# A top-k attention and MLP kernel: AV one slot later and behind the score products, the norm at the end of even slots, the MLP weights one slot later

## The chip, the cores and the metric

The kernel runs on one core of a Trainium2 chip. A core has a matrix engine (PE, or TensorE, with its weight loads shown as PEld), VectorE (DVE), ScalarE (ACT), GpSimd (POOL) and SyncE (SP), which only issues DMAs here. Each engine works through its own instructions in the order of the program and waits on semaphores for the others. The metric is the time of the whole program on the device, in microseconds (us).

## The reference: what is computed

Eight batches of eight heads, sequence 576, head dimension 64. Each row of scores keeps its 32 largest entries, softmax runs over those, and the result is multiplied by v. The eight heads side by side (512 columns) go through a two-layer MLP with a leaky activation whose slope is learned per column.

```python
scores = scale * np.matmul(q, k.transpose(0, 1, 3, 2))
kth = np.partition(scores, -top_k, axis=-1)[..., -top_k:-top_k + 1]
scores = np.where(scores >= kth, scores, -1000000000.0)
attn = np.exp(scores - np.max(scores, axis=-1, keepdims=True))
attn = attn / (np.sum(attn, axis=-1, keepdims=True) + 1e-09)
x = np.matmul(attn, v)          # (8, 8, 576, 64), then heads side by side: (4608, 512)
h = x @ w_in                    # (512, 2048)
g = np.maximum(h, 0.0) + alpha * np.minimum(h, 0.0)
out = g @ w_out                 # (2048, 512)
```

## The kernel before

Two heads make a pair (32 pairs, four to a batch). Work is cut into 144 **duos**. A normal duo is 128 rows of q of both heads of a pair, that is 256 rows of 576 scores in a tile s of 128 partitions x 2 x 576. A mixed duo takes the 64 rows left at the end of two pairs; two of each eighteen duos of a batch are mixed (the list is built at lines 77 to 85).

The main loop (line 719) goes through **slots** n = 0 to 147. Each slot emits one stage of several duos, so that a duo passes through the engines over some eight slots. The order of the calls in the loop body is the order in which each engine finds its work; nothing reorders it, apart from DVE's smallest instructions.

- Slot n computes the score products of duo n+1 on PE (`st_qk`, line 233) into the one score tile of PSUM, and ACT copies them out (`st_exit`, line 255, called the exit).
- DVE finds the eight largest of each sixth of the rows of duo n (`dve_slot`, line 313: twelve MAX8 per duo). In odd slots it folds them into a lower threshold for the two duos of the slot pair (`threshold_steps`, line 285).
- ACT takes the sign of duo n−2's scores against that threshold and counts (`st_count`), POOL makes y from it (`st_y`), and DVE takes the eight next candidates of each row from y (`row`, line 282). In even slots three small steps (`pick_steps`, line 265) pick the exact threshold of the pair two before.
- ACT and POOL then push the scores below the threshold of duo n−4 far down (`st_relu`), ACT takes exp of duo n−5 into w, and SP starts a transposing DMA of w into wT (`st_exp`, line 419 on); wT has three buffers.
- PE multiplies wT with v (`st_av`, line 426): ten matmuls for a normal duo, twenty for a mixed one. Column 64 of v is one, so that the row sums come out beside the product. The result of an even duo and the odd one behind it share the tile xo, of which there is **one** (`ps_x`, line 101). In the slot table (line 381 on) AV stands six slots behind the duo's own; it is called late in the loop body (line 751), behind the MLP part `o_pe` and the transposes of the next q and k (`prep`).
- The norm of a pair of duos (line 451) is a reciprocal of the row sums (`norm_a`) and a multiply that writes x in bf16 (`norm_b`). It is done in even slots, for the duos n−8 and n−7 (`norm_of`, line 260). Within the slot it goes: the twelve maxima with the pick steps between them, one MLP evacuation (`h_dve`), `norm_a`, first rows of y, `norm_b`, second rows. `norm_b` frees xo for the next AV, which in an even slot is that of duo n−6.
- Behind the loop body SP transposes a finished x into xT (`st_xT`), and from two slots later the MLP takes it: `h_pe` emits one unit of the first layer, at the head of a slot, `o_pe` a part of the second. Where there is no such unit, `keep_warm` (line 557, `rest` in the profile) multiplies zeros in its place.

The MLP's weights come in during the first slots: four loads of w_out and four of w_in by POOL's queue (lines 656 to 658), scaled copies of w_out by alpha on ACT and DVE (`scale_out`, line 660), transposes of w_in by SP (`in_trans`), and a product of the two (`lin`, `lin_out`) in slots 15 to 23. The first MLP unit needs the second of these products, the first output all four. All of that goes by a table of slots (`at`).

DMAs are issued in order on each queue: SP has the loads of q, k and v, the transposes of w, x and w_in, and the stores; POOL has the weights.

Of the kernel before, what the change touches and what calls it, by code (L numbers as in the profile page):

```python
# [59 lines left out]
def fast_path(tc, q, k, v, moe_w_in, moe_w_out, moe_alpha, out, flag):  # L60
# [17 lines left out]
    for b in range(B):  # L78
        p0 = KPB * b
        last = b == B - 1  # L80
# [3 lines left out]
    ND = len(duos)  # L84
# [3 lines left out]
    with ExitStack() as ctx:  # L88
# [91 lines left out]
        def at(slot, kind, f):  # L180
            todo.setdefault((max(0, slot), kind), []).append(f)
# [100 lines left out]
        def row(d, i):  # L282
            DVE.max(out=T["p9", d // 2][:, 2 * (d % 2) + i, 1:9], in_=T["y", d][:, i, :])
# [29 lines left out]
        def dve_slot(n, f_late):  # L313

            norm = norm_of(n)
            rows = [d for d in duos_at("row", n)]
            picks = [f for m in duos_at("pick", n) for f in pick_steps(m)]
            if on(n):
                s = T["s", n]
                if n % 2 == 0:  # L320
                    T["up", n // 2] = two.tile([128, 4, NG // 2, 8], FP32, name="up", tag="up")
                up = T["up", n // 2]
                for i in range(2):
                    r = 2 * (n % 2) + i
                    for g in range(NG):
                        o = 24 * r + 8 * (g // 2)
                        m = DVE.max(out=(lo if g % 2 else up)[:, r, g // 2, :],
                                    in_=s[:, i, GW * g:GW * g + GW])
                        if g % 2:
                            sm(m, [], [(o, o + 8)])  # L330
                            if picks:
                                picks.pop(0)()
                if n % 2 == 0:
                    h_dve()
                    if norm:
                        norm_a(norm)
                    for d in rows:
                        row(d, 0)
                    if norm:
                        norm_b(norm)  # L340
                    for d in rows:
                        row(d, 1)
                else:
                    fold, negate, least, turn = threshold_steps(n // 2)
                    fold()
                    h_dve()
                    negate()
                    for d in rows:
                        row(d, 0)
                    least()  # L350
                    turn()
                    for d in rows:
                        row(d, 1)
            else:
                if norm:
                    norm_a(norm)
                    norm_b(norm)
                early = picks and duos_at("pick", n)[0] < ND // 2 - 1
                if early:
                    for f in picks:  # L360
                        f()
                if not norm:
                    h_dve()
                for d in rows:
                    row(d, 0)
                    row(d, 1)
                if not early:
                    for f in picks:
                        f()
                if norm:  # L370
                    h_dve()
            if f_late:
                h_pe()
                h_dve()

        stage = {}

        def duos_at(kind, n):
            return stage.get((kind, n), [])

        for d in range(ND):
            last = d - (ND - 4) if d >= ND - 4 else None
            for kind, lag, drain in (("count", 2, (2, 2, 2, 1)), ("relu", 4, (4, 3, 3, 2)),
                                     ("exp", 5, (5, 4, 4, 3)), ("av", 6, (6, 5, 5, 4))):
                stage.setdefault((kind, d + (lag if last is None else drain[last])), []).append(d)
        for (kind, n), l in list(stage.items()):
            if kind == "count":
                stage["row", n] = l
# [174 lines left out]
        def h_dve():  # L563
            if act:
                ch, f0, e_n, ph = act.pop(0)
                DVE.tensor_scalar(ch["g"][:, f0:f0 + e_n, :], ph, 0.0, None, ALU.max)
                ch["done"] += e_n
# [48 lines left out]
        def w_in_load(i):  # L616
            POOL.dma_start(w_in_b[i], moe_w_in[128 * i:128 * i + 128, :])
# [3 lines left out]
        def out_load(i):  # L621
            hold["st", i] = gp.tile([128, 4, DMODEL], FP32, name="w_st", tag="gT")
            POOL.dma_start(hold["st", i], moe_w_out[512 * i:512 * i + 512, :].rearrange("(f p) n -> p f n", p=128))

        def scale_out(f):
            if f % 8 == 0:
                hold["wl", f // 8] = gp.tile([128, 8, 512], BF16, name="w_la", tag="gT")
            src = hold["st", f // 4][:, f % 4, :]
            ACT.activation(w_out_b[f // 4][:, f % 4, :], src, AF.Copy, scale=alpha1m[:, f:f + 1])

            sm(DVE.tensor_tensor(hold["wl", f // 8][:, f % 8, :], src,
                                 alpha_ps[:, f:f + 1].to_broadcast([128, 512]), ALU.mult),
               [(304 + f, 305 + f)], [])

        def in_trans(kk):
            if kk % 2 == 0:
                hold["wi", kk // 2] = gp.tile([128, NFT, 256], BF16, name="w_inT", tag="gT")
            SP.dma_start_transpose(hold["wi", kk // 2][:, :, 128 * (kk % 2):128 * (kk % 2) + 128], w_in_b[kk])
# [11 lines left out]
        def lin_out(kk):  # L650
            ACT.copy(w_lin_b[kk], hold["z"])
            if kk == 3:
                lin_done.append(1)


        for i in range(4):
            at((1, 3, 5, 8)[i], "w", lambda i=i: out_load(i))
            at((4, 7, 10, 12)[i], "w", lambda i=i: w_in_load(i))
        for f in range(NFT):
            at((3, 3, 4, 4, 5, 6, 7, 7, 8, 9, 10, 11, 11, 12, 13, 14)[f], "scale", lambda f=f: scale_out(f))  # L660
        for kk in range(4):
            at((11, 12, 15, 17)[kk], "ld", lambda kk=kk: in_trans(kk))
            for a in range(2):
                at(15 + 2 * kk + a, "lin", lambda kk=kk, a=a: lin(kk, a))
            at(17 + 2 * kk, "lin_out", lambda kk=kk: lin_out(kk))

        def run(n, kind, most=99):
            l = todo.get((n, kind), [])
# [50 lines left out]
        for n in range(ND + 4):  # L719
            end = n >= ND  # L720
            now[0] = n
            run(n, "ld")
            o_sp()

            if end:
                for m in duos_at("av", n):
                    st_av(m)
            if not h_pe() and not end:
                keep_warm()
            if n and on(n + 1):  # L730
                st_qk(n + 1)
            late = len(hq) > (9 if n < 118 else 4) and n % 2 == 0 or end

            for m in duos_at("count", n):
                st_count(m)
                st_y(m)
            for m in duos_at("exp", n):
                st_exp(m)
            did = o_pe()
            run(n, "w")  # L740

            dve_slot(n, late)
            for m in duos_at("relu", n):
                st_relu(m, 0)
                st_relu(m, 1)
            if on(n + 1):
                st_exit(n + 1)
            run(n, "cast")
            run(n, "lin_out")
            run(n, "prep", 2 if n < 4 else 1)  # L750
            if not end:
                for m in duos_at("av", n):
                    st_av(m)
            if end or ready() > 4 or all(len(d.shape) == 3 for d, _ in pend):
                o_act()
            if (n, "lin") in todo:
                run(n, "lin")
            else:
                late_o[0] = 0 if end else 1
                if not (end or ready() > 2) or not o_pe():  # L760
                    if not end and not did:
                        keep_warm()
                late_o[0] = 0
            while pend:
                short = len(pend[0][0].shape) == 3
                wide = pend[0][0].shape[1] == 512
                on_dve = short and n > 16 or wide and (n < 17 or n % 2 == 0)
                prep_evac(DVE.tensor_copy if on_dve else ACT.copy)
            if n == 1:
                sm(DVE.tensor_copy(alpha_ps, aps), [], [(304, 320)])  # L770
                ACT.activation(alpha1m, aps, AF.Copy, scale=-1.0, bias=1.0)
            run(n, "scale")
            if norm_of(n):
                st_xT(norm_of(n) - 1)
                st_xT(norm_of(n))
            if n == ND + 3:
                check_low()
# [294 lines left out]
```

## Time and profile before

| | us |
|---|---|
| median of three runs | 882.73 |
| lowest and highest of them | 881.53, 884.63 |
| the profiled execution's own time | 883.55 |
| its span in the profile | 881.3 |

| engine | busy us | share of the span |
|---|---|---|
| PE | 773.3 | 88% |
| DVE | 764.1 | 87% |
| ACT | 765.5 | 87% |
| POOL | 755.6 | 86% |

The mean granted clock of PE is 0.943 of full speed. A row of the timeline gives the start, the duration, the engine, the operation with what it writes and reads, how many instructions are merged in it, and in brackets how long the engine was idle before it and what ended that. A row of waits gives who waited for whom, the total, how often, and the longest. In a row of stretches each engine's busy time is followed by the count of its instructions, and then come the granted clock, the DMA engines' busy share and their GB/s. Every instruction carries the line of a helper (L32), so that groups are told apart by the tiles' names: ps_sc are the score products, s_sb the exits (by ACT) or the scores, xo is AV, x the norm's product, KZ<-xo its reciprocal, ph and gT the first MLP layer, pz the second, tps the transposes of q and k, rest the fillers.

### The profile page before, as it was taken

Reading aid. Unit: us, or ns where it says so; the run is one execution under the profiler, and the core shown is the slowest. Engines: PE = TensorE matmul, PEld = TensorE weight load, DVE = VectorE, ACT = ScalarE, POOL = GpSimd, SP = SyncE. Lnnn points to the kernel's source line nnn. Section 1 sums busy time; section 2 is a strip of 40 time slices with the busy share of each in tenths; the row PEclk is TensorE's granted clock in tenths of the full one; section 3 lists DMA queues with packets and bytes.
Section 4 is the critical chain, followed back from the end, with each engine's and each line's share of the span. In section 5 each row is a group of like instructions: output and inputs, shape, how many; then the busy total and the mean of one; then the engine's idle time right before and its main releaser. Section 6 shows DMA issues by size and latency. Waiting matters only on the chain.

```text
span 881.3 us, 17690 instructions
## 1 busy us (share of the span) xinstructions
PE 773.3 (88%) x5299; PEld 438.1 (50%) x5386; DVE 764.1 (87%) x3475; ACT 765.5 (87%) x1255; POOL 755.6 (86%) x708
## 2 busy tenths in 40 slices
PE   7858698988999889899989889899989989889887
PEld 4323254555555555455545555555545555445454
DVE  2889698999998989999997989999997989999832
ACT  3679699999998999999998989999997988998930
POOL 1589699999998999999898889999998888998930
PEclk9979799999999999997998999999998999989989
DMA  7587866556655556565554455656555554443341
GB/s 169 122 160 161 159 110 130 101 115 127 112 117 113 111 92 142 113 126 115 111 120 100 104 110 127 120 124 127 116 114 116 105 106 99 84 83 71 80 96 40
DMA packets 344167, 100.19 MB, mean 114 GB/s; under 512 B 338032, under 2 KB 338048, under 8 KB 344064
## 3 DMA queue, kind: packets, MB, share of 16 engines
q1 hardware_dynamic: 340992, 91.87, 52.1%
q0 software_dynamic: 1872, 6.82, 3.3%
q8 instruction: 44, 0.72, 0.4%
q14 instruction: 59, 0.48, 0.2%
q10 hardware_dynamic: 1200, 0.30, 0.2%
HBM read 36.71 MB, written 9.44 MB: 52 GB/s over the span
## 4 chain that ended last, share of the span: by engine, by line
PE 36%; DVE 29%; ACT 14%; POOL 10%; issue 5%; DMA 4%; SPq 1%; ACTq 0%; POOLq 0%
PE ps_sc L32 10%; PE pz L32 10%; DVE small L32 9%; DVE p L32 7%; PE ph L32 7%; DVE up L32 5%; PE xo L32 5%; POOL s_sb L32 5%; POOL y L32 4%; ACT sg L32 4%; ACT s_sb L32 4%; DVE gT L32 3%; PE rest L32 3%; ACT r L32 3%; ACT w L32 2%
## 5 line engine op out<-in xcount | busy, mean ns | idle before, releaser
L32 POOL TENSOR_TENSOR y<-s_sb,sg 128x576 f32<-128x576 f32 x288 | 361.9, 1277 | 89.6 <-ACT sg L32 88.8
L32 POOL TENSOR_TENSOR s_sb<-s_sb,r 128x576 f32<-128x576 f32 x288 | 362.0, 1277 | 1.6 <-ACT r L32 1.5
L32 DVE MAX8 up<-s_sb 128x8 f32<-128x96 f32 x864 | 212.6, 246 | 18.9 <-ACT s_sb L32 18.4
L32 ACT ACTIVATE sg<-s_sb,p 128x576 bf16<-128x576 f32 x288 | 221.1, 772 | 5.4 <-DVE p L32 4.9
L32 DVE MAX8 p<-y 128x8 f32<-128x576 f32 x288 | 215.2, 747 | 10.2 <-POOL y L32 9.7
L32 DVE MAX8 small<-s_sb 128x8 f32<-128x96 f32 x864 | 216.6, 251 | 0.0
L32 ACT COPY s_sb<-ps_sc 128x1152 f32<-128x1152 f32 x144 | 159.5, 1108 | 60.1 <-PE ps_sc L32 59.1
L32 ACT ACTIVATE r<-s_sb,KZ 128x576 bf16<-128x576 f32 x288 | 205.9, 765 | 0.0
L32 PE MATMUL ps_sc<-qkT 64*128 64x512 f32 (+2 forms) x768 | 186.1, 583 | 3.5 <-ACT s_sb L32 3.5
L32 PE MATMUL xo<-v,wT 128*128 128x65 bf16 (+3 forms) x1600 | 129.0, 201 | 67.7 <-DVE x L32 47.1
L32 ACT ACTIVATE w<-s_sb 128x1152 bf16<-128x1152 f32 x144 | 166.2, 1154 | 6.2 <-POOL s_sb L32 6.0
L32 PE MATMUL ph<-xT,w_in_b 128*128 128x256 bf16 (+1 forms) x1408 | 161.4, 265 | 0.9 <-PE xo L32 0.5
L32 PE MATMUL pz<-w_out_b,gT 128*128 128x512 bf16 x557 | 152.3, 396 | 5.6 <-issue 3.2
L32 PEld LDWEIGHTS <-wT 128*128 128x128 bf16 (+3 forms) x1600 | 97.4, 101 | 113.2 <-issue 57.4
L32 PEld LDWEIGHTS <-w_in_b 128*128 128x128 bf16 x1408 | 121.5, 103 | 38.0 <-issue 9.5
L32 DVE TENSOR_SCALAR gT<-ph 128x512 bf16<-128x512 f32 x144 | 97.7, 679 | 36.9 <-PE ph L32 36.2
L32 PEld LDWEIGHTS <-gT 128*128 128x128 bf16 x576 | 57.7, 100 | 65.3 <-issue 15.0
L32 PEld LDWEIGHTS ps_sc<-kd,qkT 128*128 128x128 f32 x256 | 38.4, 189 | 100.6 <-issue 99.0
L32 PEld LDWEIGHTS ps_sc<-qkT 64*128 64x128 f32 (+1 forms) x768 | 54.8, 175 | 59.3 <-issue 43.1
L32 PE MATMUL rest<-idle 128*128 128x512 bf16 x209 | 62.7, 421 | 4.7 <-DVE qkT L32 2.7
L32 PE MATMUL ps_sc<-kd,qkT 128*128 128x128 f32 x256 | 62.9, 328 | 0.0
L32 ACT ACTIVATION_READ_ACCUMULATOR sg<-s_sb,p 128x1 f32 x288 | 55.7, 193 | 0.0
(57 smaller groups left out, 558.8 us busy)
## 6 DMA issues: line engine op xcount, KB each, us to landing
k_st<-in_k_dram SPq DMA_DIRECT2D x64, 128.0 KB, 2.9
v_st<-in_v_dram SPq DMA_DIRECT2D x64, 128.0 KB, 2.8
q_st<-in_q_dram SPq DMA_DIRECT2D x62, 128.0 KB, 2.7
out_dram<-o_sb SPq DMA_DIRECT2D x31, 256.0 KB, 2.5
w_st<-in_moe_w_out_dram POOLq DMA_DIRECT2D x4, 1024.0 KB, 6.6
wT<-w SPq DMA_TRANSPOSE x144, 3.5
w_in_b<-in_moe_w_in_dram POOLq DMA_DIRECT2D x4, 512.0 KB, 6.2
k_st<-in_k_dram SPq DMA_DIRECT2D x32, 32.0 KB, 3.1
```

What stands on the lines that cost most here:

```text
L32: ins = self.tc.keep_in_program_order(f(*a, **kw))
```

## The change

AV of a duo stands seven slots behind the duo instead of six, and is called right behind the score products of the next duo, ahead of everything else that PE does in the slot from there on. The AV of an odd duo, n−7, thus comes in the even slot n, that of the next even duo in the odd slot n+1. The last four duos keep their slots, and no AV of the others goes beyond slot 145. In even slots DVE does the first rows of y, then `norm_a`, the second rows, then `norm_b`. All table entries of the weights (loads, scaled copies, transposes, product) go up by one slot; the slot of the norm and the MLP's own rules stay.

```diff
                 if n % 2 == 0:
                     h_dve()
+                    for d in rows:
+                        row(d, 0)
                     if norm:
                         norm_a(norm)
                     for d in rows:
-                        row(d, 0)
+                        row(d, 1)
                     if norm:
                         norm_b(norm)
-                    for d in rows:
-                        row(d, 1)
...
-                                     ("exp", 5, (5, 4, 4, 3)), ("av", 6, (6, 5, 5, 4))):
-                stage.setdefault((kind, d + (lag if last is None else drain[last])), []).append(d)
+                                     ("exp", 5, (5, 4, 4, 3)), ("av", 7, (6, 5, 5, 4))):
+                at_slot = d + (lag if last is None else drain[last])
+                if d < ND - 4:
+                    at_slot = min(at_slot, ND + 1)
+                stage.setdefault((kind, at_slot), []).append(d)
...
-            at((1, 3, 5, 8)[i], "w", lambda i=i: out_load(i))
-            at((4, 7, 10, 12)[i], "w", lambda i=i: w_in_load(i))
+            at((2, 4, 6, 9)[i], "w", lambda i=i: out_load(i))
+            at((5, 8, 11, 13)[i], "w", lambda i=i: w_in_load(i))
         for f in range(NFT):
-            at((3, 3, 4, 4, 5, 6, 7, 7, 8, 9, 10, 11, 11, 12, 13, 14)[f], "scale", lambda f=f: scale_out(f))
+            at((4, 4, 5, 5, 6, 7, 8, 8, 9, 10, 11, 12, 12, 13, 14, 15)[f], "scale", lambda f=f: scale_out(f))
         for kk in range(4):
-            at((11, 12, 15, 17)[kk], "ld", lambda kk=kk: in_trans(kk))
+            at((12, 13, 16, 18)[kk], "ld", lambda kk=kk: in_trans(kk))
             for a in range(2):
-                at(15 + 2 * kk + a, "lin", lambda kk=kk, a=a: lin(kk, a))
-            at(17 + 2 * kk, "lin_out", lambda kk=kk: lin_out(kk))
+                at(16 + 2 * kk + a, "lin", lambda kk=kk, a=a: lin(kk, a))
+            at(18 + 2 * kk, "lin_out", lambda kk=kk: lin_out(kk))
...
             if n and on(n + 1):
                 st_qk(n + 1)
+            if not end:
+                for m in duos_at("av", n):
+                    st_av(m)
...
             run(n, "prep", 2 if n < 4 else 1)
-            if not end:
-                for m in duos_at("av", n):
-                    st_av(m)
```

## The prediction

> **What bounds the kernel now.** I read the page first, then the chain of waits, the waits of the steady part, and last the timeline, slot by slot. The slots are those of the loop at line 719; "score products" are the six (or sixteen) matmuls of st_qk, "exit" is the copy of st_exit, AV the matmuls of st_av. All times are from the span's start.
>
> ```profile
> PE 773.3 (88%) x5299; PEld 438.1 (50%) x5386; DVE 764.1 (87%) x3475; ACT 765.5 (87%) x1255; POOL 755.6 (86%) x708
> ```
>
> Four engines are within two per cent of each other. No engine is the bound everywhere, so what counts is where one makes the other three stand still. The waits between 130 and 850 us (columns: total, times, longest) show who does:
>
> ```profile
> PE xo L32 <- DVE x L32: 43.8, 32, 2.8
> ACT s_sb L32 <- PE ps_sc L32: 36.0, 29, 3.3
> DVE gT L32 <- PE ph L32: 24.8, 28, 2.4
> DVE up L32 <- ACT s_sb L32: 10.5, 19, 1.2
> ```
>
> PE waits 32 times for DVE's norm (x) before the AV of an even duo: there is one xo tile, and the norm of the pair before must have read it. ACT waits 29 times for score products. These belong together, as slots 78 and 79 show, on PE, DVE and ACT:
>
> ```profile
> 461.05 0.49 PE L32 MATMUL ps_sc<-kd,qkT 128*128 128x128 f32 x2
> ...
> 464.25 1.04 PE L32 MATMUL xo<-v,wT 128*128 128x65 bf16 x10 [2.44 <-DVE x L32]
> ...
> 469.17 2.84 PE L32 MATMUL ps_sc<-qkT 64*64 64x512 f32 x16
> ```
>
> ```profile
> 462.96 0.17 DVE L32 RECIPROCAL KZ<-xo 128x4 f32<-128x4 f32 x1
> 463.05 0.72 DVE L32 MAX8 p<-y 128x8 f32<-128x576 f32 x1
> 463.70 0.40 DVE L32 TENSOR_TENSOR x<-xo,KZ 128x256 bf16<-128x256 f32 x1
> 464.02 0.75 DVE L32 MAX8 p<-y 128x8 f32<-128x576 f32 x1
> ...
> 469.28 0.69 DVE L32 TENSOR_SCALAR gT<-ph 128x512 bf16<-128x512 f32 x1 [1.59 <-PE ph L32]
> ```
>
> ```profile
> 463.52 1.10 ACT L32 COPY s_sb<-ps_sc 128x1152 f32<-128x1152 f32 x1
> ...
> 467.58 1.43 ACT L32 ACTIVATE r<-s_sb,KZ 128x576 bf16<-128x576 f32 x2
> 472.12 1.12 ACT L32 COPY s_sb<-ps_sc 128x1152 f32<-128x1152 f32 x1 [3.11 <-PE ps_sc L32]
> ```
>
> The wait of 2.44 on PE ends with x at 464.1. All that stands behind it on PE comes late by as much: the MLP unit for which DVE then waits 1.59, and the next score products, for which ACT waits 3.11. The 3.11 is more than 2.44, and the stretches around it (PE, PEld, DVE, ACT, POOL busy, granted clock, DMA share, GB/s) tell why:
>
> ```profile
> 455.00:463.70 8.70, 6.64 (x53) 3.91 (x51) 8.63 (x45) 8.63 (x15) 8.70 (x9) 1.00 0.54 104
> 463.70:470.50 6.80, 6.25 (x35) 3.60 (x37) 5.18 (x25) 5.31 (x9) 6.80 (x7) 0.50 0.67 144
> 470.50:480.00 9.50, 9.18 (x82) 5.20 (x80) 6.63 (x28) 6.93 (x12) 6.09 (x7) 1.00 0.40 74
> ```
>
> While PE waits, its clock drops to 0.50 and stays there for 6.8 us. Before the wait, DVE and ACT were busy for 8.63 of 8.70 us; behind it for some 5.2 of 6.8.
>
> **The change part by part.** The sum is made against the profiled execution, 883.55 us with a span of 881.3; the median of the three runs, 882.73, is 0.8 below, less than the runs differ.
>
> *AV later, norm at the end of even slots (steady part).* No instruction is added or taken away. The AV of an even duo now comes in the odd slot behind the score products; the norm that it waits for is at the end of the even slot before. In the rows above that norm would end at about 464.8 (the same four instructions, x last), while the products of slot 79 would begin at 469.17 − 2.44 = 466.7 at the earliest. The wait is gone, with 1.9 us and the products' own time to spare. Next in line would be the exit that the products need: it ends at 464.6, so it is no limit either. ACT could then start the exit of slot 79 at 469.01, when r ends.
>
> So each ACT wait that follows an x wait by one slot is to go. From slot 29 to 137 there are 15 of them, 26.0 us in sum; these are the first and the last, from the ACT rows:
>
> ```profile
> 195.22 1.12 ACT L32 COPY s_sb<-ps_sc 128x1152 f32<-128x1152 f32 x1 [1.46 <-PE ps_sc L32]
> ...
> 796.06 1.12 ACT L32 COPY s_sb<-ps_sc 128x1152 f32<-128x1152 f32 x1 [3.28 <-PE ps_sc L32]
> ```
>
> The bounds are 0 and the whole 36.0. I take **−26.0**, since the same slots are those in which DVE waits too. Crediting no ACT wait with more than the x wait ahead of it gives 22.4; the 3.6 between are matmuls at half clock.
>
> On that, a rule. The Trainium skill (TensorE: Matmul & The Clock Gate, Part 1: The HAM clock gate) says that the clock falls to half after an idle window of about 3.4 us. By it no x wait here, 2.8 us at most, would lower the clock, the stretches at 0.50 would stay, and the gain would be 22.4, for a time of 859.3. This trace differs from the rule's plain reading: 0.50 begins within a wait of 2.44 us; I go by the row.
>
> *The norm waits for AV.* The norm of an even slot now needs the AV of its odd duo in the same slot, behind the score products. Slot 56, in which PE is late, shows the price:
>
> ```profile
> 344.74 0.49 PE L32 MATMUL ps_sc<-kd,qkT 128*128 128x128 f32 x2
> ...
> 346.14 0.78 PE L32 MATMUL xo<-v,wT 128*128 128x65 bf16 x10
> ```
>
> ```profile
> 344.40 0.17 DVE L32 RECIPROCAL KZ<-xo 128x4 f32<-128x4 f32 x1
> 344.49 0.73 DVE L32 MAX8 p<-y 128x8 f32<-128x576 f32 x1
> ```
>
> Products end at 345.23, AV takes 0.78 and a hand-over of 0.1: 346.1. The reciprocal, moved behind one row (0.65 until the next instruction), would come at 345.05. DVE waits 1.06, and the second row, x, the evacuations and the next slot's maxima wait behind it; DVE was idle for 0.27 there, so 0.8 is left. Between slots 18 and 142 there are 63 even slots; in 32 PE waited for x, so it was ahead and AV would be done in time. The other 31 at 0.8 make 25, the upper end. The lower end is 0: DVE does the same work, so there is nothing to gain. Most of the 31 come within two or four slots of an x wait that goes, which leaves PE earlier by more than 0.8; some 10 do not. I take **+8**.
>
> *Start.* The first weight load moves from slot 1, where POOL issues it ahead of everything, to slot 2, behind POOL's first y.
>
> ```profile
> 5.47 7.68 DMA q_st<-in_q_dram
> ```
>
> ```profile
> 4.03 0.82 POOL L32 DMA_DIRECT2D w_st<-in_moe_w_out_dram  x1
> ```
>
> ```profile
> 13.28 1.09 PE L32 MATMUL tps<-ident_f,q_st 128*128 128x128 f32 x4 [3.26 <-DMA q_st<-in_q_dram]
> 14.30 2.08 PE L32 MATMUL ps_sc<-qkT 64*128 64x512 f32 x4
> ```
>
> ```profile
> 9.62 1.12 ACT L32 COPY s_sb<-ps_sc 128x1152 f32<-128x1152 f32 x1 [1.40 <-PE ps_sc L32]
> ```
>
> ```profile
> q_st<-in_q_dram SPq DMA_DIRECT2D x62, 128.0 KB, 2.7
> ```
>
> In the chain, q of the second pair takes 7.68 us beside that load of 1 MB; the median is 2.7. Without it q would be there at 8.2, and the second score products would wait only for the exit that ends at 10.74: 14.30 − 10.8 = **−3.5** (bounds 0 and 5.0, the difference of the two loads).
>
> AV of the first duo, in slot 6, waits 7.29 for its transposed weights, and the products behind it are late:
>
> ```profile
> 57.36 1.07 PE L32 MATMUL xo<-v,wT 128*128 128x65 bf16 x10 [7.29 <-DMA wT<-w]
> ```
>
> ```profile
> 63.73 1.12 ACT L32 COPY s_sb<-ps_sc 128x1152 f32<-128x1152 f32 x1 [4.42 <-PE ps_sc L32]
> ```
>
> ```profile
> 66.92 1.28 POOL L32 TENSOR_TENSOR y<-s_sb,sg 128x576 f32<-128x576 f32 x1 [4.20 <-ACT sg L32]
> ```
>
> Behind the products of slot 7 it finds them landed. What is late next is POOL, idle for 4.20: **−4.2** (0 to 4.4).
>
> In slot 12 the same happens for another reason: SP's transpose of w_in stands ahead of wT.
>
> ```profile
> 99.80 0.94 PEld L32 LDWEIGHTS <-wT 128*128 128x128 bf16 x10 [8.57 <-DMA wT<-w]
> ```
>
> ```profile
> 106.46 1.12 ACT L32 COPY s_sb<-ps_sc 128x1152 f32<-128x1152 f32 x1 [7.72 <-PE ps_sc L32]
> ```
>
> ```profile
> 92.45 1.35 SPq L32 DMA_TRANSPOSE wT<-w  x1
> 93.90 5.56 SPq L32 DMA_TRANSPOSE w_inT<-w_in_b  x1
> 99.56 1.35 SPq L32 DMA_TRANSPOSE wT<-w  x1
> ```
>
> wT was issued at 92.45 and its last piece ended PE's wait at 99.8, 7.3 later. The w_in transposes move to slots 12 and 13, so the next duo's wT takes that place on SP. Its AV comes two slots on instead of one; by the same lag it would be some 3 us late, ahead of one set of products: 7.7 − 3.0 = **−4.7** (0 to 7.7).
>
> *What else moves.* One more slot passes without MLP work, with fillers in place of it (421 ns each on the page's PE rest row, four of them: 1.7), and the 0.82 that POOL takes to issue w_st now falls where POOL is at work: **+2.5** (0 to 3).
>
> ```profile
> L32 PE MATMUL rest<-idle 128*128 128x512 bf16 x209 | 62.7, 421 | 4.7 <-DVE qkT L32 2.7
> ```
>
> At nothing I cost: x later by about 1 us on SP, since the wT behind it waits for an exp that comes later still (if not, SP's loads shift by that 1 us); wT's three buffers, each freed a slot later, as the transpose that takes one is issued a slot after its AV (a slot is 5.56 us: the exits at 195.22 and 796.06 above stand 108 slots apart); v's eight buffers, refilled a batch later; and the drain, where the last AVs keep their slots but for three that move by one, under POOL's last work.
>
> Sum: −26.0 + 8 − 3.5 − 4.2 − 4.7 + 2.5 = **−27.9**; 883.55 − 27.9 = 855.7, so **856**.
>
> **The rivals.** *Slower: DVE waits for AV instead.* PE stays late although the x waits are gone, because score products, MLP parts and transposes alone fill its slots. Then each of the 31 slots pays 0.8 (25), the 15 ACT waits stay (0), and maxima, thresholds and signs come late behind the norm. With the start's gain halved (−6.2) and 2.5: 883.55 + 25 − 6.2 + 2.5 = 905. It decides from the point at which DVE's new waits exceed 26.0 + 12.4 − 2.5 = 36, or 0.57 in each of the 63 even slots. For it: ACT also waits in 14 places that no x wait precedes (36.0 − 26.0 = 10.0). Against it: in 32 slots PE was early enough to wait. The Trainium skill (PSUM — Partial Sum Buffer, Engine vs sequencer instructions) calls VectorE's queue strict FIFO, which speaks for this case; the 1.59 row above, with everything behind it late, agrees.
>
> *Only the start gains.* The x waits go, but what PE has to do in those slots sets their length all the same: of the 26.0 a sixth is kept (4) and half of the 8 paid: 883.55 − 12.4 + 2.5 − 4 + 4 = 874. For it: behind the wait PE is busy for 6.25 of 6.8 and 9.18 of 9.50 us. Against it: the first of these stretches is at half clock, and would hold some 3.1 us at full.
>
> *The change does not do what it says.* AV in the odd slot waits for the later norm just as long. Then the steady part gives 0 + 8, the start −12.4 + 2.5: 881.7, no change that a measurement tells. Against it: 464.8 is before 466.7.
>
> **How the numbers follow.** The forecast's case has 0.62, with a range of its own from 842 (ACT's whole 36.0 goes, the norm costs 4) to 867 (half of the 26.0). Only the start: 0.14. No effect: 0.06, of which 0.04 falls within 0.3%. Slower: 0.18. About 0.3% (2.6 us) is what a measurement of this kernel tells from no change. Faster by more: 0.62 + 0.14 + 0.01 = 0.77; within: 0.04; slower: 0.19. The range from 842 to 886 leaves out the worse part of the slower case and a small tail below.
>
> **What would show it.** PE's waits for x in the steady part fall from 43.8 to under 10 us; ACT's for score products from 36.0 to about 10; hardly a stretch at 0.50 between 190 and 800 us. DVE's reciprocals wait about 8 us in sum for PE xo. The second score products begin near 11 us; the 4.42 and 7.72 on ACT shrink. The prediction is wrong if the reciprocal's waits come to 30 us and more, if new PE waits for wT or ps_sc take the place of x, or if the steady slots stay at 5.56 us.

## The result and the profile after

The changed kernel takes 873.73 us (median; 868.04 to 876.41) against 882.73 of the kernel before in the same runs: a ratio of 0.9891, with a 95% interval from 0.9848 to 0.9933. That is 9 us less, where 28 less was forecast. The time went the way that was forecast, and a third of the gain came. The profiled execution took 875.80 us, 2.1 above the median, with a span of 873.7 and a mean granted clock of 0.956 (0.943 before).

The page's line of engines is all but unchanged, still four engines within three per cent of each other:

```profile
PE 773.5 (89%) x5386; PEld 434.0 (50%) x5386; DVE 763.8 (87%) x3475; ACT 766.2 (88%) x1255; POOL 755.4 (86%) x708
```

The waits between 130 and 850 us (total, times, longest), first one row of the kernel before, then those of after:

```profile
PE pz L32 <- ACT o_sb L32: 8.9, 10, 2.1
```

```profile
PE pz L32 <- ACT o_sb L32: 44.1, 21, 3.2
ACT s_sb L32 <- PE ps_sc L32: 29.1, 24, 3.3
DVE KZ L32 <- PE xo L32: 27.6, 23, 4.3
DVE gT L32 <- PE ph L32: 22.1, 26, 2.1
```

PE's 43.8 us of waiting for x are gone to the last row. In their place PE waits 44.1 us for ACT's copy of pz, the MLP's output, to o_sb (8.9 before). ACT's wait for score products, which was to fall from 36.0 to about 10, fell to 29.1; DVE's wait ahead of the reciprocal is 27.6 us instead of the 8 foreseen (10.0 of it lie behind 820 us, where the last duos run out).

Slots 78 and 79 again, on PE and on ACT:

```profile
449.79 0.78 PE L32 MATMUL xo<-v,wT 128*128 128x65 bf16 x10
...
450.50 0.22 PE L32 MATMUL tps<-ident_f,q_st 64*128 64x64 f32 x1
453.94 0.59 PE L32 MATMUL pz<-w_lin_b,xT 128*128 128x512 bf16 x1 [3.22 <-ACT o_sb L32]
...
456.03 1.91 PE L32 MATMUL ph<-xT,w_in_b 128*128 128x128 bf16 x16
457.88 2.78 PE L32 MATMUL ps_sc<-qkT 64*64 64x512 f32 x16
```

```profile
452.32 1.10 ACT L32 COPY s_sb<-ps_sc 128x1152 f32<-128x1152 f32 x1
453.31 0.58 ACT L32 COPY o_sb<-pz 128x512 f32<-128x512 f32 x1
...
460.76 1.12 ACT L32 COPY s_sb<-ps_sc 128x1152 f32<-128x1152 f32 x1 [2.96 <-PE ps_sc L32]
```

AV no longer waits, and PE has done all it may do at 450.7. Then it stands before the next pz. There is one such tile in PSUM (`ps_z`), and ACT empties it only behind the exit, the last of the slot's long operations, at 453.31. So PE moves on at 453.94, and the next score products come 3 us late for ACT, just as before. The stretches around it (PE, PEld, DVE, ACT, POOL busy, granted clock, DMA share, GB/s) are those of before too, with 6.80 us at half clock:

```profile
440.00:452.30 12.30, 9.62 (x76) 5.85 (x77) 12.23 (x54) 12.21 (x20) 12.30 (x12) 1.00 0.50 104
452.30:459.10 6.80, 5.16 (x25) 2.88 (x26) 5.28 (x26) 5.51 (x10) 6.80 (x7) 0.50 0.56 122
```

That this second wait was there before, hidden by the first, can be read from the kernel before. Behind the AV that x held until 464.25 (shown in the prediction), these rows of ACT and PE follow:

```profile
464.52 0.58 ACT L32 COPY o_sb<-pz 128x512 f32<-128x512 f32 x1
```

```profile
465.22 0.61 PE L32 MATMUL pz<-w_lin_b,xT 128*128 128x512 bf16 x1
```

The copy ends at 465.1 and pz begins at 465.22, without a wait in its row, since AV (1.04 us) fills the time from 464.1 on. Without the x wait PE would have come there some 2.4 us earlier and stood until 465.1. The same holds for 14 of the 32 slots with an x wait, 24.7 of the 43.8 us: in each the copy of pz ends about 1 us behind x. In the other 18 no copy of pz stands in the slot. Of the 19 waits for the copy between 130 and 820 us after, ten stand in slots of the 14 (24.8 of 40.5 us). Six of the others stand in odd slots in which PE waited for the copy before too, 0.7 to 1.1 us each; five of these became about twice as long (1.9 to 2.3 us).

**Where the time went by stages.** I divide the span at the starts of two of ACT's exits, those of duos 21 and 140. The rows are those of before, then those of after:

```profile
145.07 1.12 ACT L32 COPY s_sb<-ps_sc 128x1152 f32<-128x1152 f32 x1 [0.48 <-PE ps_sc L32]
...
806.07 1.10 ACT L32 COPY s_sb<-ps_sc 128x1152 f32<-128x1152 f32 x1
```

```profile
131.84 1.10 ACT L32 COPY s_sb<-ps_sc 128x1152 f32<-128x1152 f32 x1
...
797.15 1.10 ACT L32 COPY s_sb<-ps_sc 128x1152 f32<-128x1152 f32 x1
```

| us | before | after | difference | forecast |
|---|---|---|---|---|
| start, to the exit of duo 21 | 145.1 | 131.8 | −13.2 | −12.4 |
| steady, to the exit of duo 140 | 661.0 | 665.3 | +4.3 | −18.0 (−26.0 + 8) |
| from there to the end | 75.2 | 76.5 | +1.3 | |
| span | 881.3 | 873.7 | −7.6 | |

The forecast's +2.5 for the later weights belongs to the start or the steady part. The gain is all in the start. Each row is one execution. Up to the exit of duo 21 the kernel before is the same as two of the kernels below (the rule and the copy first, each without the change), where that exit comes at 148.59 and 143.99; the changed kernel is the same as four of them, with 129.39 to 131.97. The gain of the start is thus 12 to 19 us from trace to trace. The steady part is nearer from trace to trace: 661.7 and 665.4 us in two more kernels with AV moved, 659.6 in one with AV as before.

### The profile page after: what moved, and what is told of

Same layout as the page of the kernel before. It is cut to its first block, busy times and chain, and to the rows that moved or that the text cites. A ratio compares the mean times of both kernels' runs of the same rounds, so it can differ in the third digit from the quotient of the medians.

```text
span 873.7 us, 17781 instructions
## 1 busy us (share of the span) xinstructions
PE 773.5 (89%) x5386; PEld 434.0 (50%) x5386; DVE 763.8 (87%) x3475; ACT 766.2 (88%) x1255; POOL 755.4 (86%) x708
## 4 chain that ended last, share of the span: by engine, by line
PE 41%; ACT 21%; DVE 18%; POOL 8%; issue 7%; DMA 4%; SPq 0%; ACTq 0%; POOLq 0%; DVEq 0%
PE pz L32 13%; PE ps_sc L32 11%; PE ph L32 7%; ACT sg L32 6%; ACT r L32 6%; DVE small L32 6%; PE xo L32 5%; ACT s_sb L32 5%; POOL y L32 4%; DVE p L32 4%; POOL s_sb L32 4%; DVE up L32 3%; ACT w L32 3%; DMA wT<-w 3%; PE rest L32 2%
## 5 line engine op out<-in xcount | busy, mean ns | idle before, releaser
L32 PE MATMUL ph<-xT,w_in_b 128*128 128x256 bf16 (+1 forms) x1408 | 158.6, 263 | 1.6 <-ACT qkT L32 1.0
L32 PE MATMUL pz<-w_out_b,gT 128*128 128x512 bf16 x576 | 158.0, 398 | 2.3 <-DVE gT L32 2.3
L32 PEld LDWEIGHTS <-w_in_b 128*128 128x128 bf16 x1408 | 123.9, 102 | 43.2 <-issue 11.1
L32 PE MATMUL pz<-w_lin_b,xT 128*128 128x512 bf16 x144 | 57.2, 397 | 44.1 <-ACT o_sb L32 44.1
```

The costliest lines, as they stand in the source:

```text
L32: ins = self.tc.keep_in_program_order(f(*a, **kw))
```

## The experiments

The theory after the result: PE's wait for the copy of pz has taken the place of the wait for x, and keeps both the length of the slots and the half clock behind it. The rivals: DVE's wait for AV ahead of the norm (27.6 us) gives back what the x wait gave; or PE's own work sets the slots; or the half clock does.

### Which part of the change does what

**The weights alone** (e1): the kernel before with only its weight tables one slot later, as in the change's diff.

> The kernel before with the weight tables alone moved up by one slot; AV and the norm stay. My theory of the start: of the 13 us that the changed kernel is ahead at slot 20, the part of the second q load (3.5 to 4.5 us) comes from the weights alone, and the waits of AV on wT (7.29 in slot 6, 8.57 in slot 12) stay or move. So 877 to 880 us, and at slot 20 it is 3 to 5 us ahead of the kernel before. Rival (the weights give the whole start): 869 to 871 us, 13 us ahead at slot 20.

Measured: 878.6 us, ratio 0.9975 (0.9956 to 0.9994), as the theory had it. The exit of duo 2 starts at 17.96 instead of 22.94, 5.0 us earlier; at duo 21 2.9 are left. In the five traces with the weights at their old slots this exit starts at 21.39 to 25.57, in the eight with them moved at 17.78 to 18.41. The waits for wT, the transposed w of the attention, stay in sum, since AV stands where it was, and one is longer: 14.9 us pass between the exits of duos 7 and 8, 10.2 before. PE's weight loads for AV, up to 130 us, before and here:

```profile
PEld L32 <- DMA wT<-w: 17.1, 4, 8.6
```

```profile
PEld L32 <- DMA wT<-w: 19.9, 5, 10.5
```

**AV and norm alone** (e2): the changed kernel with its weight tables put back.

> The changed kernel with the weights at their old slots. Theory: the two waits on wT at the start go (9 us), the second q load stays slow; in the steady part the waits of PE for ACT o_sb (44 us) and of the reciprocal for AV (28 us) are as in the changed kernel. So some 4 us slower than the changed kernel: 877 to 880 us. Rival (the weights give the whole start): 885 to 890 us, slower than before.

Measured: 875.74 us, 0.9936 (0.9911 to 0.9962), a little less than either case. At the exit of duo 21 it is 8.7 us ahead of before (136.4), and its steady part is 661.7 us, that of before. With the 2.9 of the weights alone that makes 11.6 of the 13.2: within what the traces differ, the two parts of the start's gain add up, and nothing comes from the steady part.

**The norm back** (e3): AV and weights changed, the norm's place in the slot as before.

```diff
-                    for d in rows:
-                        row(d, 0)
                     if norm:
                         norm_a(norm)
                     for d in rows:
-                        row(d, 1)
+                        row(d, 0)
                     if norm:
                         norm_b(norm)
+                    for d in rows:
+                        row(d, 1)
```

> The changed kernel with the norm at its old place in the even slot, ahead of the rows. Theory: the reciprocal comes 0.65 us earlier and waits that much longer for AV in each of the late slots, so its waits grow from 35.7 to about 50 us and the time by 3 to 8 us, to 877 to 882 us. Rival (DVE's waits lie in time that it has): within 2 us of the changed kernel.

Measured: 874.38 us, 0.9919 (0.9894 to 0.9945). DVE's waits ahead of the reciprocal, 130 to 820 us, first after, then with the norm back:

```profile
DVE KZ L32 <- PE xo L32: 17.6, 19, 2.0
```

```profile
DVE KZ L32 <- PE xo L32: 32.6, 25, 2.3
```

They double nearly, by 15 us, and the time stays, as the rival had it. The norm's place is worth nothing that can be measured here, and 15 us more of these waits cost nothing: DVE has that time to spare in its slots. That they are not what holds the changed kernel is shown further by the next experiment, which leaves them as they are.

### The wait for the copy of pz

**No new pz behind a copy of the same slot** (e4, below also: the rule), in the changed kernel. In a slot in which ACT is given the copy, the slot's second output part may not be one that begins a new pz; it comes with the next slot's first call instead.

```diff
-        def o_pe():
-            if ready() and not stores:
+        def o_pe(fresh=True):
+            if ready() and not stores and (fresh or oq[0][1] != 4):
...
+                held = len(stores)
                 o_act()
+                copied = len(stores) < held
+            else:
+                copied = False
...
-                if not (end or ready() > 2) or not o_pe():
+                if not (end or ready() > 2) or not o_pe(end or not copied):
```

> The changed kernel, but where ACT has just been given the copy of pz in a slot, PE's last call of that slot does not begin the next pz; that part of the MLP's second layer comes at the next slot's call. Same work. Theory (the wait for x has been replaced by the wait of the next pz for ACT's copy, o_sb): PE's waits of pz for o_sb fall from 44 us to under 10, the stretches at half clock behind them go, ACT's waits for score products in the steady part fall from 29 to about 12, and the time falls by 10 to 20 us, to 853 to 864 us, unless the parts put off lengthen the end by up to 6 us. Rival (PE's work sets these slots, the wait is only where its slack is seen): the time stays within 3 us of the changed kernel and the idle time turns up at other PE instructions.

Measured: 845.4 us, 0.9581 (0.9542 to 0.962), 28 us below the changed kernel (27 by the ratios) with the same computation, and more than was expected. Its waits from 130 to 820 us:

```profile
DVE KZ L32 <- PE xo L32: 17.2, 15, 4.7
DVE gT L32 <- PE ph L32: 9.2, 12, 2.8
...
ACT s_sb L32 <- PE ps_sc L32: 7.9, 11, 2.4
...
PE pz L32 <- ACT o_sb L32: 1.4, 2, 1.1
```

PE's wait for the copy falls from 40.5 to 1.4, and ACT's for score products to 7.9, the figure that the prediction had for the change itself. DVE's wait for AV is as long as in after (17.2 against 17.6). Its exit of duo 140 starts here, 32.8 us ahead of after's:

```profile
764.31 1.10 ACT L32 COPY s_sb<-ps_sc 128x1152 f32<-128x1152 f32 x1
```

This also refutes that PE's own work sets the slots. One thing comes in beside the rule: where a part is put off in a slot that has had none, `keep_warm` emits its four matmuls on zeros, 308 of them in all against 228 in after. The copy first, below, has 220 and gains more, so that these fillers are not the cause.

**The same rule in the kernel before**, with the same edit.

> The kernel before, with the rule of e4 alone (no next pz right behind ACT's copy); AV, norm and weights as before. Theory (x and o_sb end at about the same time, so either wait hides the other): the wait of AV for x stays at 40 us and more in the steady part, its half clock stretches too, and the time stays within 6 us of the kernel before, 876 to 884 us. Rival (the wait for o_sb was the limit all along, and AV's place does not matter): as much as e4 gained over the changed kernel, some 28 us, to 855 us or less.

Measured: 876.16 us, 0.9912 (0.9891 to 0.9933). Without the change the rule gives 7 us, at the lower end of what was expected, and the x wait is still there, if somewhat shorter than the 40 put down (130 to 820 us):

```profile
PE xo L32 <- DVE x L32: 36.7, 35, 2.8
```

**The rule, and the norm back** (the edits of the two experiments together):

> The kernel of e4 with the norm at its old place in the even slots, ahead of the rows. With the wait for o_sb gone, PE should be early enough in most slots, but the norm then stands 0.65 us earlier in DVE's order: if the norm's move is worth something, DVE's reciprocals wait 30 us and more (17 in e4) and the time rises by 4 to 10 us over e4, to 850 to 855 us. If not, it is within 2 us of e4's 845.

Measured: 846.52 us, 0.9572 (0.9545 to 0.9599): as with the rule alone, with 22.3 us of waits ahead of the reciprocal. Also with the wait for the copy gone, the norm's place makes no difference that can be told; its waits grew by only 5 us here.

**The rule only up to slot 119**, `o_pe(end or n >= 120 or not copied)`, as the rule leaves more of the MLP for the end (80.1 us behind the exit of duo 140, against 76.5 in after):

> The kernel of e4 with its rule only up to slot 119. The parts put off make the end longer: from the last exit to the end e4 takes 58.3 us, the kernel before 53.7. With the rule off early that falls by 2 to 5 us, but the 24 slots behind it lose some 4 us to waits for o_sb: 842 to 848 us, no clear difference from e4. If parts put off cost nothing at the end, it is 3 to 5 us slower.

Measured: 844.46 us, 0.9573 (0.9533 to 0.9614). The end is 76.4 us, but the whole is no shorter by what can be told. (The last exits start at 780.50 with the rule and at 821.95 before, which makes 63.9 and 59.3 us to the end and not 58.3 and 53.7; the difference of the two is the same.)

**The copy first** (e11): the changed kernel, in which ACT copies pz at the head of its slot, ahead of the counts, and not behind the exit. The condition that let the copy wait for another slot goes too.

```diff
+            if not end:
+                o_act()
             for m in duos_at("count", n):
...
-            if end or ready() > 4 or all(len(d.shape) == 3 for d, _ in pend):
+            if end:
                 o_act()
```

> The changed kernel with ACT's copy of pz (o_sb) at the head of its slot's work instead of at its end, so that a pz finished late in one slot is copied early in the next; a next pz begins only behind that. Same work. Theory (the place of this copy in ACT's order is what holds PE): PE's waits of pz for o_sb fall under 10 us as in e4, and the time to 842 to 855 us; as against e4, parts put off are fewer, but each copy stands ahead of the signs. Rival (e4 gained by spreading the parts, not by the wait): 865 to 875 us.

Measured: 841.01 us (840.38 to 841.75), 0.9513 (0.9483 to 0.9543), the fastest of all and 1 us below what was expected. The waits from 130 to 820 us, and the stretch from 150 to 800 (columns as above):

```profile
PE ps_sc L32 <- ACT s_sb L32: 26.1, 43, 1.2
...
DVE KZ L32 <- PE xo L32: 13.0, 7, 4.6
...
PE pz L32 <- ACT o_sb L32: 7.0, 2, 6.4
...
ACT s_sb L32 <- PE ps_sc L32: 0.9, 2, 0.5
```

```profile
150.00:800.00 650.00, 599.81 (x4384) 341.73 (x4383) 627.50 (x2890) 631.25 (x1035) 629.87 (x566) 0.99 0.57 115
```

Now PE waits for ACT's exit, 43 times and never more than 1.2 us, and ACT, POOL and DVE are each busy for some 630 of 650 us. Up to 785 us no wait of an engine for another is longer than 2.6 us; the two longest of these rows stand behind that, PE's 6.4 for the copy at 793 and DVE's 4.6 for AV at 811.

**The copy first in the kernel before**, the same edit:

> The kernel before, with ACT's copy of pz at the head of its slot as in e11; AV, norm and weights as before. Theory (the waits for x and for o_sb hide each other, so that either alone gives little): the wait for x stays at 35 us and more in the steady part, and the time at 870 to 880 us; the change is then worth 30 us and more where the copy does not stand in its way (e11 has 841). Rival (the copy alone was the limit and the change adds only its start): 13 us above e11, at 852 to 858 us.

Measured: 869.13 us, 0.9891 (0.9853 to 0.9929), 1 us less than expected. The x wait stays, and so does a part of ACT's for score products (130 to 820 us):

```profile
PE xo L32 <- DVE x L32: 44.2, 41, 2.5
...
ACT s_sb L32 <- PE ps_sc L32: 14.7, 15, 3.2
```

The four kernels, as ratios to the kernel before:

| | AV, norm and weights as before | changed |
|---|---|---|
| copy of pz behind the exit | 1 | 0.9891 (0.9848 to 0.9933) |
| copy of pz first | 0.9891 (0.9853 to 0.9929) | 0.9513 (0.9483 to 0.9543) |

Two independent gains would give 0.9891 x 0.9891 = 0.978. Measured is 0.951, so each is worth much more where the other has been made: the change 9 us with the copy behind the exit, and 869.1 − 841.0 = 28 us with the copy first (33 by the ratios, as the runs of before beside the two differ). With the rule in place of the copy first it is 876.2 − 845.4 = 31 us (29). So the two waits of PE, for x and for the copy, hide each other: with either one left, PE is held all the same.

### The clock behind the wait

**Fillers before the waiting pz**: the changed kernel with eight matmuls on zeros in the slots where pz would wait for a copy of the same slot. They add nothing to the output.

```diff
+            if copied and not end and ready() > 2 and oq[0][1] == 4:
+                fill = ps_h.tile([128, 512], FP32, name="rest", tag="h")
+                for i in range(8):
+                    PE.matmul(fill, idle[:, 0:128], idle, start=(i == 0), stop=(i == 7))
```

> The changed kernel, with eight matmuls on zeros put ahead of each next pz that waits for ACT's copy in the same slot (1.7 us of the wait filled, no other order changed). The wait itself stays as long in sum with the filling. If the half clock behind the wait has a price of its own, the stretches at half clock between 150 and 800 us shrink from 48 us to 20 and the time falls by 4 to 9 us, to 865 to 870 us. If only the wait counts, the time stays within 2 us of the changed kernel or rises.

Measured: 861.18 us, 0.9763 (0.9741 to 0.9784). PE in the place of the 3.22 above, and the waits from 130 to 820 us:

```profile
445.58 1.89 PE L32 MATMUL rest<-idle 128*128 128x512 bf16 x7 [1.16 <-DVE gT L32]
447.63 0.38 PE L32 MATMUL pz<-w_lin_b,xT 128*128 128x512 bf16 x1 [0.17 <-ACT o_sb L32]
```

```profile
PE rest L32 <- DVE gT L32: 18.2, 24, 2.0
ACT s_sb L32 <- PE ps_sc L32: 15.7, 18, 3.3
...
PE pz L32 <- ACT o_sb L32: 6.2, 11, 3.2
```

PE gets past pz no sooner, it only works meanwhile: from the start of AV to that of pz 4.14 us pass here (AV at 443.49) and 4.15 in after. But its clock is full. The stretch from 150 to 800 us, before, after, and with the fillers; the mean granted clock is the third figure from the end:

```profile
150.00:800.00 650.00, 590.23 (x4066) 336.96 (x4134) 605.59 (x2799) 608.08 (x993) 603.88 (x545) 0.95 0.55 112
```

```profile
150.00:800.00 650.00, 588.95 (x4134) 333.75 (x4133) 603.10 (x2783) 604.68 (x987) 599.39 (x541) 0.96 0.54 110
```

```profile
150.00:800.00 650.00, 605.75 (x4317) 346.73 (x4380) 614.21 (x2834) 617.03 (x1006) 612.62 (x551) 1.00 0.56 112
```

In stretches of half a microsecond, 61, 48 and 3 us of the 650 are at half clock. So of the 28 us between the changed kernel and the one without the wait, 873.7 − 861.2 = 12.5 (11.3 by the ratios), more than the 4 to 9 expected, come from the half clock behind the wait, less what the fillers cost. The kernel without the wait is 16 us faster still, though it has more half clock (20 us): these are the wait itself, and what the fillers may cost; matmuls on zeros wait 18.2 us in sum for DVE to free their place in PSUM, 7.8 in after. How the 16 split is not shown.

**Fillers ahead of AV in the kernel before**, the same eight matmuls in every slot whose AV is that of an even duo, from slot 17 on, where PE often waits for x:

```diff
                 for m in duos_at("av", n):
+                    if m % 2 == 0 and n > 16:
+                        fill = ps_h.tile([128, 512], FP32, name="rest", tag="h")
+                        for i in range(8):
+                            PE.matmul(fill, idle[:, 0:128], idle, start=(i == 0), stop=(i == 7))
                     st_av(m)
```

> The kernel before, with eight matmuls on zeros (1.7 us) ahead of each AV of an even duo, that is in the wait for x (from slot 17 on). If half clock behind a short wait has a price in the kernel before too, its stretches at half clock between 150 and 800 us fall from 61 us to under 20 and the time by 5 to 12 us, to 870 to 877 us, though the fillers also stand in some 30 slots where PE did not wait for x and cost there up to 1.7 us each. If the price was the wait alone, the time rises by 5 to 30 us.

Measured: 912.72 us, 1.0322 (1.0289 to 1.0354). The clock is full here too (1.00 from 150 to 800 us), and it is slower by 29 us (912.72 − 883.30). Two of its waits, 130 to 820 us, show why:

```profile
POOL y L32 <- ACT sg L32: 71.3, 64, 4.7
ACT s_sb L32 <- PE ps_sc L32: 63.2, 59, 3.8
```

The fillers (1.89 us for eight) stand in every second slot, whether PE would have waited there or not, and AV and the score products stand behind them. ACT's wait for products goes up by 27 us, from 36.0 in the same stretch before. Of the two cases put down this is the one in which the wait alone has a price, but the run can't decide it: the fillers also stand in about as many slots without a wait, and how much the full clock gave back in this kernel can't be told from it.

## Why the prediction was right and wrong

*The start: right in the sum, in part by luck.* −13.2 against −12.4, where the traces give 12 to 19. The terms were off both ways: 5.2 up to duo 2 for 3.5, 1.8 around slot 7 for 4.2, 7.2 around slot 12 for 4.7. By the starts of the exits of duos 2, 8, 14 and 21, the changed kernel is ahead by 5.2, 10.6, 15.0 and 13.2 us. The second score products begin at 10.22 instead of 14.30 (4.1 against the 3.5 of the sum):

```profile
10.22 1.13 PE L32 MATMUL ps_sc<-qkT 64*128 64x512 f32 x4 [0.34 <-ACT s_sb L32]
```

Between the exits of duos 7 and 8 it gains 4.2, as the sum had it, and between those of 13 and 14 7.2 instead of 4.7. A part of it comes back at AVs that still wait for their transposed weights, in slots where they now stand:

```profile
54.68 1.06 PE L32 MATMUL xo<-v,wT 128*128 128x65 bf16 x10 [4.17 <-DMA wT<-w]
...
101.85 2.27 PE L32 MATMUL xo<-v,wT 128*64 128x65 bf16 x20 [2.12 <-DMA wT<-w]
```

"Behind the products of slot 7 it finds them landed" was thus wrong: 4.17 us are left. The exit of duo 9, behind that AV, is 8.1 us ahead of before, 2.4 less than the exit of duo 8.

*The x waits: right that they go, wrong on what they are worth.* They fell from 43.8 to nothing. The step that failed is the sentence on what is late next: "Next in line would be the exit that the products need: it ends at 464.6, so it is no limit either." It looked at what the score products wait for, and not at everything that stands on PE between AV and them. There stands pz, which needs ACT's copy, and the copy comes right behind the very exit that was called no limit and ends 0.5 us after it. From the rows of before, PE's next start would have been 465.1 instead of 465.22 in that slot, a gain of some 0.1 and not of 2.4. In the sum the step is the term −26.0: the steady part of after is no shorter than before (665.3 against 661.0 us). The exit itself, the other half of that sentence, was rightly called no limit in slot 79. Of the signs of being wrong that the prediction names, one came true: the steady slots stay at 5.56 us (5.59 after). The wait that took the place of x, for o_sb, is not among those it names (PE's wait ahead of ps_sc, which is, came to 10.6 us).

*The size of −26.0* was too large even without that obstacle. From the exit of duo 21 to that of duo 140 the steady part is 661.0 us before and 634.9 in the changed kernel with the rule, a difference of 26.1. But the rule alone takes it to 647.9 in the kernel before, so that the change is worth 13.0 on top of it; with the copy first it is 646.5 and 630.4, or 16.1. The rest of the difference, 19 and 12 us, lies ahead of the exit of duo 21, where the sum had 12.4; neither edit acts there yet, so that 19 and 12 differ only as executions do. That the 15 ACT waits belong to the x waits was right only for the pair of waits together: removing both took ACT's wait for products to 7.9 or 0.9.

*The +8 for the norm: wrong in both ways.* The waits ahead of the reciprocal were longer (27.6 us), and with 15 us more of them the time stayed. So the rival that ends slower had the sign of DVE's new wait right, but 27.6 is below its own point of decision, 36, and the kernel with the rule has about as much of them from 130 to 820 us and takes 28 us less. What such a wait costs depends on whether the engine is late for another.

*The clock: right by the row.* The Trainium skill (TensorE: Matmul & The Clock Gate, Part 1: The HAM clock gate) speaks of an idle window of about 3.4 us; by its plain reading no x wait would have cost clock. In after the longest wait for pz is 3.2 us, 0.50 is granted for 6.80 us around one of 3.22, and filling most of such waits brought the mean from 0.96 to 1.00 and gave 12.5 us. That stretches at 0.50 would hardly be left did not come true (48 us of the 650 after, 61 before). The same section says that the window runs freely and that activity in it is what counts, which would allow this; how busy it must be no run here shows. Its consequence for the forecast, that the stretches at 0.50 stay, came true for another reason: a new wait took the old one's place.

*The rival "only the start gains"* gives 874, which is the time measured, by luck. That only the start gains is right; its mechanism, PE's own work setting the slots, is refuted by the two kernels that take 28 and 33 us less with the same computation.

*The things costed at nothing* (SP's order, the buffers of wT and v) showed no waits of PE for wT from 130 to 820 us; SP waits there for AV, 7.0 us in six pieces, as it did not before. The end is 1.3 us longer.

## What to carry to other kernels

Before crediting a removed wait, walk down the waiting engine's own order from there to the instruction whose lateness is the cost, and ask for each one in between when its operands and its buffer come free: two waits of one engine that end at nearly the same time hide each other, and taking away one gave 7 to 12 us here where taking away both gave 36 and 42. A PSUM tile of which there is only one ties the engine that fills it to the place of the copy that empties it; moving that copy up in its engine's order gave 33 us in the changed kernel and 12 in the one before. 15 us more of waits on an engine that was ahead cost nothing, while waits of PE of some 2 us each cost in two ways, as time and as clock.

## What the runs showed of the hardware

PE's waits for pz are 2.1 us long on the mean (44.1 in 21) and 3.2 at most. That the half clock behind them costs some 12 of the 28 us that go with these waits was not expected in this size; the fillers show it. They are no remedy everywhere: put ahead of every even AV of the kernel before, they gave the full clock too, and cost 29 us in sum. And the loads of the weights moved by one slot brought the exit of duo 2 5.0 us forward, while the whole gained 2.7.
